# Holding back loads by TensorE progress, and moving transposes to the DMA queues, in a linear-attention and SwiGLU kernel

## The chip, the cores and the metric

One core of one Trainium2 chip runs the whole program. The metric is device microseconds of one execution. The kernel before takes 787.03 us (median of 3 runs, 786.19 to 787.52). Different chips of the same kind gave the same kernel 788.6 to 790.0 us, so every experiment is compared with runs of the kernel before made on the same chip beside it.

## The reference, cut to what matters

```python
xn = layernorm(x)                      # x: 2048 x 1024
# A: linear attention, 32 heads of 32
q, k, v = split(xn @ wqkv)
pq, pk = phi(q), phi(k)                # phi(t) = t + 1 or exp(t), + 1e-6
kv, z = pk^T v, sum(pk)
s = ((pq kv) / (pq z)) @ wo
# B: SwiGLU, 1024 -> 3584 -> 1024
g = silu((silu(xn @ w_gate) * (xn @ w_up)) @ w_down)
return x + s * g
```

The tolerance is not an issue here.

## The kernel before

TensorE computes the large products by a seven-product scheme on 2x2 blocks, so VectorE (DVE) has to form sums of weight blocks ("combinations") before the products, and DVE and ScalarE (ACT) have to empty PSUM, the memory that takes TensorE's products, between them. All instructions are first recorded as operations with their regions. A planner then simulates the five engines and a DMA model and writes each engine's instruction stream in the simulated order. That order is fixed: each engine executes its own stream in order, so an instruction that waits holds everything behind it on that engine. The queue on SyncE (SP), which issues all DMAs, is such a stream too.

The parts that the change touches, with cuts marked:

```python
# Planner: deadline of each op, and the DMA model of the simulation
for o in reversed(ops):
    d = o.pecum if o.eng == "pe" else o.pecum + 30.0     # pecum: TensorE work recorded before it
    for s in o.succs:
        extra = (2.5 + o.nbytes / 250e3) if o.sem is not None else o.busy + o.lat
        d = min(d, s.dl - extra)
    o.dl = d - o.urgent
...
    b = max(s + 0.7, dma_free)
    dma_free = b + o.nbytes / 300e3
    o.done = dma_free + 1.4

# stage 1: each of 16 x tiles (128 x 1024) is normalised, then transposed by TensorE
def t_tile(i):
    ...
    pe_tr([s.r, ident_r], [bank_r[MISC]], trs)           # 8 transposes of 128x128
    act([bank_r[MISC]], [xt_r(i)], dst, pb[:, :, :], ACT.Identity)

# last stage, 8 sets: g*s is 128 columns x 512 tokens, transposed before it is added to x
def turn():
    pe_tr([g.r, ident_r], [bank_r[MISC]], ...)           # 4 transposes of 128x128
    tt([bank_r[MISC], q.r], [q.r], xv[...], pb, xv[...], ALU.add)
    ...                                                  # store when both halves are there
defer(2, turn)

# after the second gate/up pair: 1/denominator is stored to r_scratch, read back
# broadcast in rows of 256 elements, and multiplied into all 16 tiles of phi(q) at once
if (k, n) == ("g", 1):
    recip(p)
    normalise(p)
```

Of the kernel before, what the change touches and what calls it, by code (L numbers as in the profile page):

```python
# [8 lines left out]
ACT = mybir.ActivationFunctionType  # L9
# [4 lines left out]
KB = 1024  # L14
# [15 lines left out]
class Plan:  # L30
# [3 lines left out]
    ENGS = ("pe", "act", "dve", "pool", "sp")  # L34
    LAT = {"pe": 0.22, "act": 0.2, "dve": 0.2, "pool": 0.2}

    def __init__(self, window):
        self.ops = []
        self.lastw = {}
        self.readers = {}  # L40
        self.pecum = 0.0
        self.window = window

    def op(self, eng, reads, writes, fn, busy, sem=None, nbytes=0, urgent=0.0, cow=None):

        o = Op()
        o.eng, o.fn, o.busy, o.sem, o.nbytes, o.urgent = eng, fn, busy, sem, nbytes, urgent
        o.lat = 0.0 if sem is not None else self.LAT[eng]
        o.idx = len(self.ops)
        preds = set()  # L50
        for r in reads:
            for k in r.keys:
                preds.update(self.lastw.get(k, ()))
        if cow is not None:
            preds.update(cow.preds)
        for r in writes:
            for k in r.keys:
                if cow is None:
                    preds.update(self.lastw.get(k, ()))
                    preds.update(self.readers.get(k, ()))  # L60
        for r in reads:
            for k in r.keys:
                self.readers.setdefault(k, []).append(o)
        for r in writes:
            for k in r.keys:
                if cow is None:
                    self.lastw[k] = [o]
                    self.readers[k] = []
                else:
                    self.lastw[k].append(o)  # L70
        o.preds = preds
        o.succs = []
        for p in preds:
            p.succs.append(o)
        o.pecum = self.pecum
        if eng == "pe":
            self.pecum += busy
        self.ops.append(o)
        return o

    def schedule(self):
        ops = self.ops
        for o in reversed(ops):
            d = o.pecum if o.eng == "pe" else o.pecum + 30.0
            for s in o.succs:
                extra = (2.5 + o.nbytes / 250e3) if o.sem is not None else o.busy + o.lat
                d = min(d, s.dl - extra)
            o.dl = d - o.urgent
        for o in ops:
            o.npred = len(o.preds)  # L90
            o.ready = 0.0
# [10 lines left out]
        while len(order) < total:  # L102
# [26 lines left out]
            o.start = s  # L129
            if o.sem is not None:  # L130
                free[e] = s + 0.08
                b = max(s + 0.7, dma_free)
                dma_free = b + o.nbytes / 300e3
                o.done = dma_free + 1.4
            else:
                free[e] = s + o.busy
                o.done = s + o.busy + o.lat
# [65 lines left out]
    return last  # L203


def build_kernel(nc, A_x, A_wqkv, A_wo, B_w_gate, B_w_up, B_w_down, out, WINDOW=6, NWARM=14):
    S, D, FF = 2048, 1024, 3584
    NT, KT, NG, NPAIR = 16, 8, 8, 14
    EPS_LN, EPS_PHI = 1e-5, 1e-6
# [9 lines left out]
    with ExitStack() as es:  # L219
# [42 lines left out]
        m_scr = nc.dram_tensor("m_scratch", [D, D], FP16)  # L262
        m_v = m_scr.rearrange("(g p) c -> p g c", p=128)
        q_scr = nc.dram_tensor("q_scratch", [2, 2, 2, 128, 4 * 512], FP16)
        r_scr = nc.dram_tensor("r_scratch", [2, 4, 32, 256], BF16)

        ps = [es.enter_context(nc.psum_tensor("ps%d" % b, [128, 512], F32)) for b in range(8)]
        bank_r = [named("bank", b) for b in range(8)]
# [17 lines left out]
                semn[name] = sem("d_" + name)  # L286
            return semn[name]

        PL = Plan(WINDOW)
        MM = 0.2137  # L290

        def mm_cost(mms):
# [21 lines left out]
        def tt(reads, writes, o, a, b, op, fast=False):  # L314
            return dve(reads, writes, lambda h: h.tensor_tensor(o, a, b, op), nel(o), 1.92 if fast else 0.96)  # L315

        def dma(reads, writes, o, i, s, nbytes, cow=None):
            return PL.op("sp", reads, writes, lambda h: h.dma_start(o, i), 0.08, sem=s, nbytes=nbytes, cow=cow)  # L318

        class Ring:  # L320
            def __init__(self, arena, off, size, n):
# [59 lines left out]
        rr_ring = Ring(TM, 18 * KB, 2 * KB, 3)  # L381
        fin_ring = Ring(TM, 10 * KB, 1 * KB, 8)
        xo_ring = Ring(TM, 18 * KB, 2 * KB, 3)
        x_ring = Ring(W, 32 * KB, 2 * KB, 4)
        xn_ring = Ring(W, 40 * KB, 2 * KB, 2)
        pk_ring = Ring(W, 44 * KB, 2 * KB, 2)
# [44 lines left out]
        def x_load(i):  # L431
            s = x_ring.take()
            xslot[i] = s
            dma([], [s.r], s.ap(), xf[i * 128:(i + 1) * 128, :], dsem("x%d" % s.k), 256 * KB)

        def wkv_load(c):
            dma([], [wkv_r[c]], wkv[c], wqkv_v[:, :, 1024 + c * 512:1024 + (c + 1) * 512], dsem("wkv%d" % c), 1024 * KB)
# [28 lines left out]
        def t_tile(i):  # L466
            s = xnslot[i]
            xa = s.ap(FP16)
            ar, j, m = xt_dest(i)
            pb = ps[MISC][:, :].bitcast(FP16).rearrange("p (k t) -> p k t", t=128)  # L470
            trs = [(pb[:, kt, :], xa[:, kt * 128:(kt + 1) * 128], ident[:, :]) for kt in range(KT)]
            pe_tr([s.r, ident_r], [bank_r[MISC]], trs)
            dst = ar.at(j * 8 * KB, 8 * KB, FP16).rearrange("p (k t) -> p k t", t=512)[:, :, m * 128:(m + 1) * 128]
            act([bank_r[MISC]], [xt_r(i)], dst, pb[:, :, :], ACT.Identity)
# [287 lines left out]
        def recip(p):  # L762

            flush()
            db = den[p][0]
            e = rr_ring.take()
            ea, ra, rb = e.ap(F32, 0, KB), e.ap(F32, KB, KB), e.ap(BF16, 0, KB // 2)
            er, rr = e.sub(0, KB).r, e.sub(KB, KB).r
            dve([bank_r[db]], [er], lambda h: h.tensor_scalar(ea, ps[db][:, 0:256], 16.0, EPS_PHI, ALU.mult, ALU.add), 256)
            rearm(db)  # L770
            for q in range(4):
                dve([er], [e.sub(KB + q * 256, 256).r], lambda h, q=q: h.reciprocal(
                    ra[:, q * 64:q * 64 + 64], ea[:, q * 64:q * 64 + 64]), 400)
            act([rr], [er], rb, ra, ACT.Identity, "sb")
            dma([er], [named("rscr", p)], r_scr[p].rearrange("q h t -> (q h) t"), rb, dsem("rs"), 64 * KB)

        RB0 = 68 * KB

        def normalise(p):

            for j in range(2):
                rb = H.at(RB0 + j * 8 * KB, 8 * KB).rearrange("p (g q t) -> p g q t", g=NG, q=2)
                rbr = H.reg(RB0 + j * 8 * KB, 8 * KB)
                first = None
                for hl in range(4):
                    rows = r_scr[p, 2 * j:2 * j + 2, :, :].rearrange("q (g h) t -> h g q t", h=4)[hl]
                    for q in range(2):
                        o0 = dma([named("rscr", p)], [rbr], rb[32 * hl:32 * hl + 32, :, q, :],
                                 rows[:, q, :].partition_broadcast(32), dsem("rr%d_%d_%d" % (j, hl, q)), 128 * KB, first)
                        first = first or o0  # L790
                for g in range(NG):
                    src, sr = pq_tile(g, j)
                    dst = src.bitcast(FP16)
                    o = RB0 + j * 8 * KB + g * KB
                    zr, zrr = H.at(o, KB), H.reg(o, KB)
                    act([z_r, zrr], [zrr], zr, zr, ACT.Identity, "sb", scale=zc[:, g:g + 1])
                    tt([sr, zrr], [sr], dst, src, zr, ALU.mult, True)
            for j in range(2):
                for k in range(2):
                    o = PQ0 + (2 * k + j) * 4 * KB  # L800
                    dma([H.reg(o, 4 * KB)], [named("q", p, k, j)], q_scr[p, k, j], H.at(o, 4 * KB, FP16),
                        dsem("pq%d%d" % (k, j)), 512 * KB)


        HB = 6 * KB
# [11 lines left out]
        def gu_load(n):  # L817
            return wload([wg_v[:, :, n * 256:(n + 1) * 256], wu_v[:, :, n * 256:(n + 1) * 256]])

        def gu_pair(p, n, stat):  # L820
            sgs = {}

            def ev_g(i, j, ap, r, bank):
# [4 lines left out]
            def ev_u(i, j, ap, r, bank):  # L828
                s = sgs[i, j]
                o, orr = hb(n, "R%d%d" % (i, j))  # L830
                tt([r, s.r], [orr], o, ap, s.ap(FP16), ALU.mult)
            run_pair(xset(stat, 0, XV[p], ev_g, d_ring), xset(stat, 1, XV[p], ev_u, d_ring))
            if n % 2 == 1:
                v = {nm: hb2(n - 1, nm) for nm in HOF}
                tt([v["R11"][1], v["R01"][1]], [v["T3"][1]], v["T3"][0], v["R11"][0], v["R01"][0], ALU.subtract, True)
# [67 lines left out]
        def d_set(p, c, Sx, mstat, first):  # L903
            gv, sv, xo = {}, {}, {}

            def fin(i, j):
# [11 lines left out]
                q, seen = xo[j]  # L918
                xv = q.ap().rearrange("p (m n) -> p m n", n=256)

                def turn():
                    half = tcnt[0] % 2
                    tcnt[0] += 1
                    pb = ps[MISC][:, half * 256:half * 256 + 256].bitcast(FP16).rearrange("p (m n) -> p m n", n=128)
                    pe_tr([g.r, ident_r], [bank_r[MISC]], [(pb[:, m, :], g.ap(FP16)[:, m * 128:(m + 1) * 128], ident[:, :])
                                                           for m in range(4)])
                    tt([bank_r[MISC], q.r], [q.r], xv[:, :, i * 128:i * 128 + 128], pb[:, :, :],
                       xv[:, :, i * 128:i * 128 + 128], ALU.add)
                    seen.append(i)
                    if len(seen) == 2:  # L930
                        dma([q.r], [], of[row:row + 512, c * 256:(c + 1) * 256].rearrange(
                            "(m p) n -> p m n", p=128), xv, dsem("oo%d" % q.k), 256 * KB)
                defer(2, turn)

            def keep(store, func):
                def f(i, j, ap, r, bank):
# [59 lines left out]
        for p in range(2):  # L996
            for k, n in order:
# [1 line left out]
                if k == "q":  # L999
                    q_pair(p, n, st, ((1, kv_done), (9, kvt)) if (p, n) == (0, 0) else ())  # L1000
                else:
                    gu_pair(p, n, st)
                pump(2)
                if p == 0 and n < 2 and k == "g":
                    for _ in range(8):
# [1 line left out]
                            m_build(*mb.popleft())  # L1007
                if (k, n) == ("g", 1):
                    recip(p)
                    normalise(p)  # L1010
            pq_load(p)
            for c in range(4):
                Sx = wd_load(c)
# [76 lines left out]
```

## Time and profile before

| | before |
|---|---|
| time, median of 3 | 787.03 us |
| span of the profiled run | 787.9 us |
| TensorE busy | 763.0 us, 97% |
| matmuls and transposes on TensorE | 3818 |
| granted TensorE clock, mean | 0.999 |

From the page of the kernel before: busy time by engine, then busy tenths in 40 slices of the span (one digit per 19.7 us), then the chain of work that ended last.

```profile
PE 763.0 (97%) x3818; PEld 347.7 (44%) x3818; DVE 513.2 (65%) x945; ACT 305.0 (39%) x507; POOL 11.5 (1%) x33
PE   8999999999999999999999999999999999999997
DVE  5587432768597766886365676788776768557353
DMA  9921000232883233370633623279423242251510
PE 81%; DMA 10%; ACT 4%; DVE 3%; SPq 2%; issue 1%; ACTq 0%
```

TensorE is the limit. Busy time alone can't say how much is left to win, because matmuls overlap in their records: each 128x512 matmul is shown as 379 ns, though the next starts 216 ns later. So I priced TensorE by start-to-start distances in the records: 216 ns for a matmul of 512 columns, 56 ns for a 128x128 transpose, 59 ns for 129 columns, 219 ns for two 32-row denominator matmuls side by side. The sum is **P = 752.3 us**. The span is then 1.4 us before the first matmul, P, the **gaps G = 30.8 us** (first matmul to last, less P), and 3.4 us after the last.

From the waits of the kernel before (engine, line, what was waited for: us in total, times, longest):

```profile
DVE W L315 <- DMA W<-in_B_w_down_dram: 34.3, 8, 7.7
DVE W L315 <- DMA W<-in_B_w_up_dram: 25.0, 8, 4.8
PE ps L195 <- DVE ps L315: 5.5, 6, 1.4
PE ps L195 <- ACT ps L308: 4.1, 3, 1.5
```

DVE stands 59 us behind weight loads. That is harmless as long as nothing behind it in the stream is wanted. From the timeline (start us, duration us, and in brackets the idle time before and what ended it), one place where something was:

```profile
672.63 5.13 PE L195 MATMUL ps<-H,W 128*128 128x512 f16 x23
677.19 1.28 DVE L315 TENSOR_TENSOR W<-W 128x896 f16<-128x896 bf16 x2 [3.63 <-DMA W<-in_B_w_down_dram]
678.39 0.69 DVE L315 TENSOR_TENSOR ps<-ps,TM 128x512 f32<-128x512 f32 x1
679.14 1.69 PE L195 MATMUL ps<-H,W 128*128 128x512 f16 x7 [1.38 <-DVE ps L315]
```

DVE waited 3.63 us for a load of w_down to form a combination that was wanted only later; the PSUM addition behind it in the stream came late, and TensorE stood 1.38 us for that addition.

Two more places. Near 40 us TensorE waits for a transpose of an x tile that was loaded late, because weight loads filled the queues (DMA share 0.98 and 0.93): the load of x tile 4 was issued at 29.2 us and landed at 36.5 us. And the normalisation: DVE and ACT work through 16 tiles in a lump near 213 to 228 us and again near 530 us. First a line of the timeline, then rows of the windows view (stretch, its length, busy us and count of each engine, granted clock, DMA share, GB/s):

```profile
41.33 0.62 PE L202 MATMUL ps<-ident,W 128*128 128x128 f16 x8 [1.32 <-DVE veps L449]
```

```profile
0.00:20.00 20.00, 16.58 (x83) 7.45 (x84) 11.14 (x26) 6.85 (x9) 4.39 (x20) 1.00 0.98 310
20.00:40.00 20.00, 20.00 (x117) 9.96 (x114) 10.61 (x24) 7.57 (x13) 0.91 (x2) 1.00 0.93 268
...
195.00:250.00 55.00, 51.84 (x242) 22.83 (x241) 42.60 (x77) 31.55 (x58) 0.00 (x0) 1.00 0.67 179
```

### The profile page before, as it was taken

The numbers are of one execution on the slowest core, as the hardware profiler recorded it, in microseconds if no ns is written. First come the engines' busy times: TensorE is split into PE (matmuls) and PEld (weight loads), VectorE is DVE, ScalarE is ACT, GpSimd is POOL, SyncE is SP. The second block draws the span as 40 slices with busy tenths as digits, with TensorE's granted clock in tenths as the row PEclk, the third lists the DMA queues.
The fourth block names the chain that finished last, engine by engine and source line by source line (L and its number), as shares of the span: only waits on it lengthen the run. The fifth ranks groups of instructions, "written<-read, shape, count | busy, mean of one in ns | idle before, by whom it ended". The sixth has DMA issues, their size and how long they took to land.

```text
span 787.9 us, 9684 instructions
## 1 busy us (share of the span) xinstructions
PE 763.0 (97%) x3818; PEld 347.7 (44%) x3818; DVE 513.2 (65%) x945; ACT 305.0 (39%) x507; POOL 11.5 (1%) x33
## 2 busy tenths in 40 slices
PE   8999999999999999999999999999999999999997
PEld 3445555444434444444444444344444444444443
DVE  5587432768597766886365676788776768557353
ACT  3344443555573334322222245547333332232131
POOL 2020000000000000000000000000000000000000
PEclk9999999999999999999999999999999999999999
DMA  9921000232883233370633623279423242251510
GB/s 310 277 67 41 1 1 1 81 107 63 190 246 106 73 89 106 94 222 9 197 92 82 183 71 96 66 156 296 143 63 106 76 126 62 59 171 50 154 41 27
DMA packets 142893, 86.74 MB, mean 110 GB/s; under 512 B 3328, under 2 KB 138752, under 8 KB 142848
## 3 DMA queue, kind: packets, MB, share of 16 engines
q1 hardware_dynamic: 142848, 86.13, 38.8%
q8 instruction: 30, 0.49, 0.3%
q14 instruction: 15, 0.12, 0.1%
HBM read 75.50 MB, written 10.62 MB: 109 GB/s over the span
## 4 chain that ended last, share of the span: by engine, by line
PE 81%; DMA 10%; ACT 4%; DVE 3%; SPq 2%; issue 1%; ACTq 0%
PE ps L195 79%; DMA W<-m_scratch 4%; ACT H L308 2%; PE ps L202 2%; SPq L318 2%; DMA H<-in_A_wqkv_dram 1%; DMA W<-in_B_w_down_dram 1%; DMA H<-r_scratch 1%; DVE W L315 1%; DMA W<-in_B_w_up_dram 1%; ACT TM L308 1%; DVE ps L315 1%; DMA m_scratch<-H 0%; DVE TM L315 0%; ACT ps L308 0%
## 5 line engine op out<-in xcount | busy, mean ns | idle before, releaser
L195 PE MATMUL ps<-X,W 128*128 128x512 f16 x1504 | 346.7, 379 | 7.7 <-DVE TM L315 2.8
L308 ACT ACTIVATE TM<-ps 128x512 f32<-128x512 f32 (+2 forms) x300 | 177.0, 596 | 302.6 <-PE ps L195 302.2
L195 PEld LDWEIGHTS ps<-X,W 128*128 128x128 f16 (+1 forms) x1504 | 143.4, 98 | 184.5 <-DVE ps L315 5.7
L315 DVE TENSOR_TENSOR W<-W 128x1024 f16<-128x1024 bf16 (+3 forms) x224 | 137.3, 629 | 73.2 <-DMA W<-in_B_w_down_dram 34.3
L195 PE MATMUL ps<-H,W 128*128 128x512 f16 x672 | 153.3, 379 | 4.2 <-DVE ps L315 4.0
L195 PE MATMUL ps<-P,W 128*128 128x512 f16 x512 | 122.9, 379 | 1.5 <-ACT ps L308 1.5
L195 PEld LDWEIGHTS ps<-H,W 128*128 128x128 f16 (+1 forms) x672 | 64.7, 98 | 82.2 <-DVE ps L315 7.1
L315 DVE TENSOR_TENSOR ps<-ps,TM 128x512 f32<-128x512 f32 x80 | 55.6, 695 | 69.5 <-PE ps L195 69.5
L315 DVE TENSOR_TENSOR TM<-ps,TM 128x512 f32<-128x512 f32 (+1 forms) x112 | 68.2, 610 | 36.5 <-PE ps L195 27.0
L308 ACT ACTIVATE ps<-ps 128x512 f32<-128x512 f32 x80 | 47.0, 587 | 101.2 <-PE ps L195 101.0
L195 PEld LDWEIGHTS ps<-P,W 128*128 128x128 f16 (+1 forms) x512 | 49.2, 98 | 60.8 <-ACT ps L308 2.0
L315 DVE TENSOR_TENSOR H<-ps,TM 128x512 f16<-128x512 f32 x84 | 57.4, 685 | 4.7 <-PE ps L195 3.3
L195 PE MATMUL ps<-H,X 128*128 128x512 bf16 x256 | 57.3, 379 | 2.6 <-ACT X L308 1.8
L195 PE MATMUL ps<-H,P 128*128 128x512 bf16 x256 | 56.6, 379 | 0.0
L308 ACT ACTIVATE TM<-TM 128x512 f16<-128x512 f32 (+1 forms) x54 | 33.5, 620 | 56.6 <-DVE TM L315 56.4
L315 DVE TENSOR_TENSOR H<-H 128x1024 f16<-128x1024 f16 (+1 forms) x74 | 41.6, 571 | 12.2 <-ACT H L308 11.2
L494 DVE TENSOR_SCALAR TM<-TM 128x512 f16<-128x512 f16 x64 | 17.9, 290 | 41.6 <-ACT TM L308 41.1
L195 PEld LDWEIGHTS ps<-H,X 128*128 128x128 f16 x256 | 24.4, 98 | 31.0 <-ACT X L308 2.1
L195 PEld LDWEIGHTS ps<-H,P 128*128 128x128 f16 x256 | 24.7, 98 | 28.3
L315 DVE TENSOR_TENSOR W<-H 128x1024 f16<-128x1024 f16 x38 | 25.4, 685 | 0.5
L308 ACT ACTIVATE H<-H,zc 128x512 bf16<-128x512 bf16 x32 | 20.8, 716 | 5.0 <-DMA H<-r_scratch 5.0
L495 DVE SCALAR_TENSOR_TENSOR W<-ps,TM 128x512 bf16<-128x512 f32 x32 | 22.0, 688 | 0.8
(60 smaller groups left out, 307.9 us busy)
## 6 DMA issues: line engine op xcount, KB each, us to landing
W<-in_B_w_gate_dram SPq DMA_DIRECT2D x28, 512.0 KB, 3.9
W<-in_B_w_up_dram SPq DMA_DIRECT2D x28, 512.0 KB, 5.2
W<-in_B_w_down_dram SPq DMA_DIRECT2D x16, 896.0 KB, 7.1
W<-in_A_x_dram SPq DMA_DIRECT2D x16, 256.0 KB, 4.1
H<-in_A_wqkv_dram SPq DMA_DIRECT2D x4, 1024.0 KB, 8.8
W<-in_A_wqkv_dram SPq DMA_DIRECT2D x8, 512.0 KB, 7.5
TM<-in_A_x_dram SPq DMA_DIRECT2D x16, 256.0 KB, 4.2
H<-r_scratch SPq DMA_DIRECT2D x32, 128.0 KB, 4.2
```

The costliest lines, as they stand in the source:

```text
L195: last = h.matmul(o, l, r, start=st, stop=sp, skip_group_check=True)
L202: last = h.transpose(o, i, ident)
L308: return PL.op("act", reads, writes, lambda h: h.activation(o, i, func, **kw), nel(o) / 1200.0 + (0.055 if src == "ps" else 0.095))
L315: return dve(reads, writes, lambda h: h.tensor_tensor(o, a, b, op), nel(o), 1.92 if fast else 0.96)
L318: return PL.op("sp", reads, writes, lambda h: h.dma_start(o, i), 0.08, sem=s, nbytes=nbytes, cow=cow)
L494: dve([e.r], [b.r], lambda h: h.tensor_scalar(ba, ea, 1.0, EPS_PHI, ALU.min, ALU.add), 512, 2.6)
L495: dve([src_r, b.r], [out_r], lambda h: h.scalar_tensor_tensor(out_ap, src, 0.0, ba, ALU.max, ALU.add), 512)
```

## The change

The intent: take TensorE off work that the DMA queues can do, and let loads be issued by TensorE's progress instead of as early as a buffer allows. It has five parts.

```diff
 # 1. planner model: a DMA is assumed slower
-                extra = (2.5 + o.nbytes / 250e3) if o.sem is not None else ...
+                extra = (4.0 + o.nbytes / 200e3) if o.sem is not None else ...
-                b = max(s + 0.7, dma_free)
-                dma_free = b + o.nbytes / 300e3
-                o.done = dma_free + 1.4
+                b = max(s + 1.0, dma_free)
+                dma_free = b + o.nbytes / 230e3
+                o.done = dma_free + 1.8
 # 2. holding back: a DMA waits for the TensorE op that lies LEAD = 12 us before its deadline
+        for o in ops:
+            if o.sem is not None and o.succs:
+                k = bisect_right(cum, o.dl - self.lead) - 1
+                if k >= 0 and pes[k] not in o.preds:
+                    o.preds.add(pes[k])
 #    and x loads get a deadline 10 us earlier
-            dma([], [s.r], s.ap(), xf[...], dsem(...), 256 * KB)
+            dma([], [s.r], s.ap(), xf[...], dsem(...), 256 * KB).urgent = 10.0
 # 3. x tiles 4 to 15: DMA transpose
+            if i >= 4:
+                PL.op("sp", [s.r], [xt_r(i)], lambda h: h.dma_start_transpose(dst, xa), ...)
+                return
 # 4. output products of all sets but the last: DMA transpose, then an add from SBUF
+                    PL.op("sp", [g.r], [o.r], lambda h: h.dma_start_transpose(oa, g.ap(FP16)), ...)
+                    tt([o.r, q.r], [q.r], xv[...], oa, xv[...], ALU.add, True)
...
+                if (p, c) == (1, 3):
+                    defer(2, turn)
+                else:
+                    turn_dma()
 # 5. normalisation: four parts over gate/up pairs 2 and 3, rows of 512 elements;
#    the loads of its rows wait for the TensorE op recorded just before them
-                    normalise(p)
+                    if 2 <= n <= 3:
+                        at = tuple((4 + 6 * h, partial(normalise_part, p, n - 2, h)) for h in range(2))
```

More of the change, by code (lines that the diff above doesn't have):

```diff
@@ L1 @@
+from bisect import bisect_right
 from collections import deque
@@ L35, with __init__ @@
     LAT = {"pe": 0.22, "act": 0.2, "dve": 0.2, "pool": 0.2}
-    def __init__(self, window):
+    def __init__(self, window, lead):
         self.ops = []
@@ L42, in __init__, with op @@
         self.window = window
-    def op(self, eng, reads, writes, fn, busy, sem=None, nbytes=0, urgent=0.0, cow=None):
+        self.lead = lead
+    def op(self, eng, reads, writes, fn, busy, sem=None, nbytes=0, urgent=0.0, cow=None, after=None):
         o = Op()
@@ L55, in op @@
             preds.update(cow.preds)
+        if after is not None:
+            preds.add(after)
         for r in writes:
@@ L77, in op @@
             self.pecum += busy
+            self.lastpe = o
         self.ops.append(o)
@@ L85, in schedule @@
             for s in o.succs:
-                extra = (2.5 + o.nbytes / 250e3) if o.sem is not None else o.busy + o.lat
+                extra = (4.0 + o.nbytes / 200e3) if o.sem is not None else o.busy + o.lat
                 d = min(d, s.dl - extra)
             o.dl = d - o.urgent
+        pes = [o for o in ops if o.eng == "pe"]
+        cum = [o.pecum + o.busy for o in pes]
+        for o in ops:
[3 more added lines that the diff above has]
+                    o.preds.add(pes[k])
+                    pes[k].succs.append(o)
         for o in ops:
@@ L203, in _tr_group, with build_kernel @@
     return last
-def build_kernel(nc, A_x, A_wqkv, A_wo, B_w_gate, B_w_up, B_w_down, out, WINDOW=6, NWARM=14):
+def build_kernel(nc, A_x, A_wqkv, A_wo, B_w_gate, B_w_up, B_w_down, out, WINDOW=6, NWARM=14, LEAD=12.0):
     S, D, FF = 2048, 1024, 3584
@@ L264, in build_kernel @@
         q_scr = nc.dram_tensor("q_scratch", [2, 2, 2, 128, 4 * 512], FP16)
-        r_scr = nc.dram_tensor("r_scratch", [2, 4, 32, 256], BF16)
+        r_scr = nc.dram_tensor("r_scratch", [2, 2, 32, 512], BF16)
         ps = [es.enter_context(nc.psum_tensor("ps%d" % b, [128, 512], F32)) for b in range(8)]
@@ L287, in dsem @@
             return semn[name]
-        PL = Plan(WINDOW)
+        PL = Plan(WINDOW, LEAD)
         MM = 0.2137
@@ L315, in tt, with dma @@
             return dve(reads, writes, lambda h: h.tensor_tensor(o, a, b, op), nel(o), 1.92 if fast else 0.96)
-        def dma(reads, writes, o, i, s, nbytes, cow=None):
-            return PL.op("sp", reads, writes, lambda h: h.dma_start(o, i), 0.08, sem=s, nbytes=nbytes, cow=cow)
+        def dma(reads, writes, o, i, s, nbytes, cow=None, after=None):
+            return PL.op("sp", reads, writes, lambda h: h.dma_start(o, i), 0.08, sem=s, nbytes=nbytes, cow=cow,
+                         after=after)
         class Ring:
@@ L383, in build_kernel @@
         xo_ring = Ring(TM, 18 * KB, 2 * KB, 3)
+        pt_ring = Ring(TM, 24 * KB, 1 * KB, 2)
         x_ring = Ring(W, 32 * KB, 2 * KB, 4)
@@ L433, in x_load @@
             xslot[i] = s
-            dma([], [s.r], s.ap(), xf[i * 128:(i + 1) * 128, :], dsem("x%d" % s.k), 256 * KB)
+            dma([], [s.r], s.ap(), xf[i * 128:(i + 1) * 128, :], dsem("x%d" % s.k), 256 * KB).urgent = 10.0
         def wkv_load(c):
@@ L469, in t_tile @@
             ar, j, m = xt_dest(i)
+            if i >= 4:
+                dst = ar.at(j * 8 * KB, 8 * KB, FP16).rearrange("p (k t) -> p k t", t=512)[:, :, m * 128:(m + 1) * 128]
+                PL.op("sp", [s.r], [xt_r(i)], lambda h: h.dma_start_transpose(dst, xa), 0.08, sem=dsem("tx%d" % (i % 2)),
+                      nbytes=400 * KB)
+                return
             pb = ps[MISC][:, :].bitcast(FP16).rearrange("p (k t) -> p k t", t=128)
@@ L774, in recip @@
             act([rr], [er], rb, ra, ACT.Identity, "sb")
-            dma([er], [named("rscr", p)], r_scr[p].rearrange("q h t -> (q h) t"), rb, dsem("rs"), 64 * KB)
-        RB0 = 68 * KB
-        def normalise(p):
-            for j in range(2):
-                rb = H.at(RB0 + j * 8 * KB, 8 * KB).rearrange("p (g q t) -> p g q t", g=NG, q=2)
-                rbr = H.reg(RB0 + j * 8 * KB, 8 * KB)
-                first = None
-                for hl in range(4):
-                    rows = r_scr[p, 2 * j:2 * j + 2, :, :].rearrange("q (g h) t -> h g q t", h=4)[hl]
-                    for q in range(2):
-                        o0 = dma([named("rscr", p)], [rbr], rb[32 * hl:32 * hl + 32, :, q, :],
-                                 rows[:, q, :].partition_broadcast(32), dsem("rr%d_%d_%d" % (j, hl, q)), 128 * KB, first)
-                        first = first or o0
-                for g in range(NG):
-                    src, sr = pq_tile(g, j)
-                    dst = src.bitcast(FP16)
-                    o = RB0 + j * 8 * KB + g * KB
-                    zr, zrr = H.at(o, KB), H.reg(o, KB)
-                    act([z_r, zrr], [zrr], zr, zr, ACT.Identity, "sb", scale=zc[:, g:g + 1])
-                    tt([sr, zrr], [sr], dst, src, zr, ALU.mult, True)
-            for j in range(2):
-                for k in range(2):
-                    o = PQ0 + (2 * k + j) * 4 * KB
-                    dma([H.reg(o, 4 * KB)], [named("q", p, k, j)], q_scr[p, k, j], H.at(o, 4 * KB, FP16),
-                        dsem("pq%d%d" % (k, j)), 512 * KB)
@@ new lines, in recip, with normalise_part @@
+            o0 = None
+            for q in range(4):
+                t0 = (q % 2) * 256
+                o1 = dma([er], [named("rscr", p)], r_scr[p, q // 2, :, t0:t0 + 256], rb[32 * q:32 * q + 32, :],
+                         dsem("rs%d" % q), 16 * KB, o0)
+                o0 = o0 or o1
+        RB0 = 68 * KB
+        def normalise_part(p, j, half):
+            o = RB0 + (2 * j + half) * 4 * KB
+            rb, rbr = H.at(o, 4 * KB).rearrange("p (g t) -> p g t", t=512), H.reg(o, 4 * KB)
+            first = None
+            for hl in range(4):
+                rows = r_scr[p, j].rearrange("(g h) t -> h g t", h=4)[hl, 4 * half:4 * half + 4]
+                o0 = dma([named("rscr", p)], [rbr], rb[32 * hl:32 * hl + 32, :, :], rows.partition_broadcast(32),
+                         dsem("rr%d_%d_%d" % (j, half, hl)), 128 * KB, first, PL.lastpe)
+                first = first or o0
+            for gl in range(4):
+                g = 4 * half + gl
+                src, sr = pq_tile(g, j)
+                dst = src.bitcast(FP16)
+                zr, zrr = H.at(o + gl * KB, KB), H.reg(o + gl * KB, KB)
+                act([z_r, zrr], [zrr], zr, zr, ACT.Identity, "sb", scale=zc[:, g:g + 1])
+                tt([sr, zrr], [sr], dst, src, zr, ALU.mult, True)
+            o = PQ0 + (2 * half + j) * 4 * KB
+            dma([H.reg(o, 4 * KB)], [named("q", p, half, j)], q_scr[p, half, j], H.at(o, 4 * KB, FP16),
+                dsem("pq%d%d" % (half, j)), 512 * KB)
@@ L818, in gu_load, with gu_pair @@
             return wload([wg_v[:, :, n * 256:(n + 1) * 256], wu_v[:, :, n * 256:(n + 1) * 256]])
-        def gu_pair(p, n, stat):
+        def gu_pair(p, n, stat, at=()):
             sgs = {}
@@ L831, in ev_u @@
                 tt([r, s.r], [orr], o, ap, s.ap(FP16), ALU.mult)
-            run_pair(xset(stat, 0, XV[p], ev_g, d_ring), xset(stat, 1, XV[p], ev_u, d_ring))
+            run_pair(xset(stat, 0, XV[p], ev_g, d_ring), xset(stat, 1, XV[p], ev_u, d_ring), at)
             if n % 2 == 1:
@@ L919, in fin, with done, turn_dma @@
                 xv = q.ap().rearrange("p (m n) -> p m n", n=256)
+                def done():
+                    seen.append(i)
+                    if len(seen) == 2:
+                        dma([q.r], [], of[row:row + 512, c * 256:(c + 1) * 256].rearrange(
+                            "(m p) n -> p m n", p=128), xv, dsem("oo%d" % q.k), 256 * KB)
+                def turn_dma():
+                    o = pt_ring.take()
+                    oa = o.ap(FP16).rearrange("p (m n) -> p m n", n=128)
+                    PL.op("sp", [g.r], [o.r], lambda h: h.dma_start_transpose(oa, g.ap(FP16)), 0.08,
+                          sem=dsem("tp%d" % o.k), nbytes=200 * KB)
+                    tt([o.r, q.r], [q.r], xv[:, :, i * 128:i * 128 + 128], oa, xv[:, :, i * 128:i * 128 + 128], ALU.add,
+                       True)
+                    done()
                 def turn():
@@ L928, in turn @@
                        xv[:, :, i * 128:i * 128 + 128], ALU.add)
-                    seen.append(i)
-                    if len(seen) == 2:
-                        dma([q.r], [], of[row:row + 512, c * 256:(c + 1) * 256].rearrange(
-                            "(m p) n -> p m n", p=128), xv, dsem("oo%d" % q.k), 256 * KB)
-                defer(2, turn)
+                    done()
+                if (p, c) == (1, 3):
+                    defer(2, turn)
+                else:
+                    turn_dma()
             def keep(store, func):
@@ L1001, in build_kernel @@
                 else:
-                    gu_pair(p, n, st)
+                    at = ()
+                    if 2 <= n <= 3:
+                        at = tuple((4 + 6 * h, partial(normalise_part, p, n - 2, h)) for h in range(2))
+                    gu_pair(p, n, st, at)
                 pump(2)
```

## The prediction

> **What bounds it now.** TensorE: the page shows it 97% busy over a 787.9 us span, granted clock 0.999; the chain of waits is 81% TensorE. In the instruction records successive 128x512 matmuls start 216 ns apart, 128x128 transposes 56 ns. Pricing every matmul so gives about 752 us. The rest: 1.4 us before the first matmul, 3.4 us after the last, about 31 us of gaps. Of the gaps 4.6 us fall in the first 25 us; 2.3 us around 40 us (a transpose waits for a late x tile; DMA share 0.95 up to there); about 5 us at 213-228 and 530 us (normalisation: DVE and ACT work through r_scratch products while PSUM evictions wait); about 6 us around the small denominator matmuls; 4.4 us at transposes of output products; most of the remainder where in-order DVE stood behind a weight load (it waited 34 us for w_down, 25 us for w_up) and evicted late.
>
> **What the change does.**
> 1. 12 of 16 x tiles lose 8 TensorE transposes each, 28 of 32 output products 4 each: 208 x 56 ns = 11.7 us, all on the critical path. Sure gain.
> 2. The turn gaps outside the last set go: 2.5 us.
> 3. Weight loads held back free the DMA queues for x in the first 40 us: the 2.3 us gap goes. The start itself stays.
> 4. Normalisation is cut into four parts over two weight pairs, with 1024-byte rows in place of 512: 3 of its 5 us.
> 5. The planner's slower DMA model places DVE's weight combinations later in its order: perhaps 2 us.
>
> **What it adds.** 12 DMA transposes of 256 KB and 28 of 128 KB, 6.7 MB beside 86 MB. The Trainium skill ("Advanced Engine Details and Errata", X-Bar Transpose) expects 350-400 GB/s of them; no run here shows one yet. Estimate from the trace: packets up to 512 bytes take 27 ns; 64 packets of 256 bytes on each of 16 engines is 1.7 us for an x tile, plus about 2.5 us that small transfers show from issue to landing: 4 us, and 3.5 us for a product. An x tile has over 7 us of matmuls ahead of it, so its latency is hidden. The products' adds sit in DVE's in-order stream: where a transpose lands later than planned, DVE blocks and evictions slip; loads behind a transpose in the in-order queue wait for its product. I charge 3 us for this and for held-back loads that come late.
>
> **Sum.** 787 - 11.7 - 2.5 - 2.3 - 3 - 2 + 3, about 768.5 us; range 759 to 780. Faster by over 2% (below 771.3): 0.62; within 2%: 0.35; slower: 0.03.
>
> **What would show the steps right.** TensorE instructions fall by 208, clock unchanged; the gaps' sum falls from 31 to roughly 24 us; DVE waits on w_down and w_up fall from 59 us together to under 40; DMA share before 40 us falls; the gap near 40 us is gone; TensorE waits under 1 us for DMA-transposed x; transposes land in 3 to 5 us.
>
> **What would make it wrong.** DMA transposes that land in 8 us or more, or slow other transfers beside them: DVE waits for them appear in the output stages (about 330-420 and 660-790 us) with new TensorE gaps, and the gain shrinks to 5 us or none. Loads held back too far: waits on weights grow in the gate/up stages. Gaps that merely move: only the 11.7 us arrive, 775 us. If the gaps fall by more than 15 us, the time is below 760.

## More of the kernel before

G counts waits and matmuls that run at a lower clock. The document uses P and G for each kernel; they are worked out, not printed by any view.

## The result, and the profile after

The changed kernel takes **763.32 us** (median of 3 runs, 763.12 to 765.06), against 787.03. The ratio is 0.9707, 95% interval 0.9681 to 0.9732. A ratio is the mean time of one kernel's fast runs over that of the other's in the same rounds, so not quite the ratio of the medians. A second measurement on another chip gave 762.40 us and 0.9664 (0.9639 to 0.9688): two measurements of the same pair can differ by 0.4%, and I read nothing smaller out of comparisons between chips. All outputs are right.

| | before | after |
|---|---|---|
| span of the profile | 787.9 | 763.1 (second profile 760.4) |
| TensorE weight loads recorded (one for each matmul) | 3818 | 3610 |
| P, priced TensorE work | 752.3 | 740.6 |
| G, gaps from first to last matmul | 30.8 | 17.6 (second profile 14.9) |
| DVE waits for w_down and w_up | 59.3 | 0.5 |

So of 24.8 us of span, 11.7 us are work that TensorE no longer does and 13.2 us are gaps. (15 matmul records are missing from this trace, so P of after is P of before less 208 x 56 ns.)

From the page of the kernel after, the lines that answer to those above:

```profile
PE 748.0 (98%) x3595; PEld 338.8 (44%) x3610; DVE 517.6 (68%) x945; ACT 296.9 (39%) x497; POOL 11.9 (2%) x33
PE   6999999999999999999999999999999999999997
DVE  4665623868798677785574868788877778565463
DMA  9333314525385332543547554246732336337740
PE 95%; ACT 2%; DVE 1%; DMA 1%; issue 0%; SPq 0%
```

DMA fell from 10% to 1% of the chain that ended last. Waits of the kernel after:

```profile
DVE TM L329 <- DMA TM<-TM: 18.2, 10, 6.3
DVE W L329 <- DMA W<-in_B_w_up_dram: 0.5, 1, 0.5
PE ps L209 <- DMA H<-in_A_wqkv_dram: 2.2, 1, 2.2
PE ps L209 <- DVE ps L329: 1.1, 2, 0.6
```

The DVE waits for weights are gone; new ones stand for transposed products (TM<-TM), up to 6.3 us, and yet TensorE waited only 1.1 us for DVE's additions. Windows of the kernel after, for comparison with the rows above:

```profile
0.00:20.00 20.00, 13.64 (x65) 6.30 (x67) 8.38 (x20) 6.04 (x7) 4.49 (x20) 0.91 0.88 287
20.00:40.00 20.00, 19.89 (x110) 9.81 (x110) 14.06 (x35) 7.10 (x12) 2.99 (x5) 1.00 0.29 68
...
195.00:250.00 55.00, 55.00 (x257) 24.95 (x255) 45.10 (x78) 31.41 (x55) 0.00 (x0) 1.00 0.64 187
```

The DMA share between 20 and 40 us fell from 0.93 to 0.29, x tile 4 landed at 21.1 us instead of 36.5, the gap near 40 us is gone, and from 195 to 250 us TensorE has no gap. But the first 20 us got worse. Timeline of TensorE after:

```profile
7.62 0.62 PE L216 MATMUL ps<-ident,W 128*128 128x128 f16 x8 [1.62 <-DVE W L470]
10.40 2.92 PE L209 MATMUL ps<-H,X 128*128 128x512 bf16 x8 [2.15 <-DMA H<-in_A_wqkv_dram]
```

The first projection matmul waited 2.15 us for its weight and ran at half clock (8 matmuls in 2.92 us where they took 1.90 us before). Two things delayed that weight: the urgency puts the second x tile ahead of it (0.7 us), and in this profile one of the 16 DMA engines landed its share 3.5 us after the first engine. In the second profile that spread was 1.6 us, in the kernel before 0.5 us.

From the list of DMA issues after (last number: median us from issue to landing), the transposes:

```profile
TM<-TM SPq DMA_TRANSPOSE x28, 2.9
P<-W SPq DMA_TRANSPOSE x8, 3.1
X<-W SPq DMA_TRANSPOSE x4, 3.1
```

### The profile page after: what moved, and what is told of

Its sections match the earlier page's. It is cut to its first block, busy times and chain, and to the rows that moved or that the text cites. A ratio compares the mean times of both kernels' runs of the same rounds, so it can differ in the third digit from the quotient of the medians.

```text
span 763.1 us, 9351 instructions
## 1 busy us (share of the span) xinstructions
PE 748.0 (98%) x3595; PEld 338.8 (44%) x3610; DVE 517.6 (68%) x945; ACT 296.9 (39%) x497; POOL 11.9 (2%) x33
## 4 chain that ended last, share of the span: by engine, by line
PE 95%; ACT 2%; DVE 1%; DMA 1%; issue 0%; SPq 0%
PE ps L209 95%; DMA H<-in_A_wqkv_dram 1%; ACT H L322 0%; PE ps L216 0%; ACT TM L322 0%; DVE TM L329 0%; ACT L322 0%; DVE W L329 0%; DVE ps L329 0%; ACT ps L322 0%; ACT X L322 0%; SPq L332 0%; DVE H L606 0%; DVE H L516 0%; DVE zc L601 0%
## 5 line engine op out<-in xcount | busy, mean ns | idle before, releaser
L209 PE MATMUL ps<-H,W 128*128 128x512 f16 x672 | 150.6, 379 | 1.4 <-ACT TM L322 1.4
L329 DVE TENSOR_TENSOR W<-W 128x1024 f16<-128x1024 bf16 (+3 forms) x224 | 133.9, 628 | 4.7 <-PE ps L209 2.3
L329 DVE TENSOR_TENSOR TM<-ps,TM 128x512 f32<-128x512 f32 (+1 forms) x84 | 56.7, 675 | 55.4 <-PE ps L209 52.6
L329 DVE TENSOR_TENSOR TM<-TM 128x512 f16<-128x512 f16 (+1 forms) x60 | 25.1, 420 | 29.5 <-DMA TM<-TM 18.2
```

Of the source, the lines that this page charges most:

```text
L209: last = h.matmul(o, l, r, start=st, stop=sp, skip_group_check=True)
L329: return dve(reads, writes, lambda h: h.tensor_tensor(o, a, b, op), nel(o), 1.92 if fast else 0.96)
```

## The experiments

**Theory A.** Half of the gain is TensorE work that the transposes save, 11.7 us, with or without the rest; the other half is gaps that close because the new planning stops DVE and the SP queue from standing behind loads. **Rival B.** The transposes carry nearly all of the gain. **Rival C.** The new planning carries it and the transposes alone cost as much as they save.

### Each part alone, and all but the transposes

b_tr adds parts 3 and 4 to the kernel before:

```diff
 # kernel before
+            if i >= 4:   (DMA transpose of x, as in the change)
+                    turn_dma()   (DMA transpose of products, as in the change)
```

> The kernel before plus the DMA transposes alone (12 x tiles, 28 output products); no holding back, old planner model, old normalisation. Theory A (half of the gain is TensorE issue, half is gaps closed by the new planning): 208 x 56 ns = 11.7 us go, and some 2.5 us of turn waits, so about 773 us. Rival B (the transposes carry nearly all of it): about 765 us. Rival C (without the new planning the transposes cost as much as they save): 780 us or more.

a_pe_tr puts every transpose of the kernel after back on TensorE:

```diff
 # kernel after
-            if i >= 4:
+            if i >= NT:
-                if (p, c) == (1, 3):
+                if p >= 0:
```

> The kernel after with every transpose back on TensorE; holding back, new planner model and new normalisation kept. Theory A: 763.3 + 11.7 + about 2 us of turn waits, so about 777 us. Rival B: about 787 us, nothing left of the gain. Rival C: about 777 us too; it differs from A in the run before.

b_hold_model adds parts 1 and 2 to the kernel before, without the urgency:

```diff
 # kernel before
+  the slower DMA model (part 1); +  o.preds.add(pes[k]) with LEAD = 12.0 (part 2)
```

> The kernel before plus the holding back of loads and the slower planner model, nothing else. Theory A: DVE waits for w_down and w_up fall from 59 us to under 15 us and 5 to 8 us of TensorE gaps go, so 779 to 782 us. Rival B: 786 to 788 us, the waits of DVE were off the critical path.

b_norm adds part 5 to the kernel before:

```diff
 # kernel before
-                    normalise(p)
+                    normalise_part(p, n - 2, h) at two points of pairs 2 and 3; r_scratch rows of 512
```

> The kernel before plus the new normalisation alone (four parts, 1024-byte rows). Theory A: the gaps of about 5 us at 213-228 us and 530 us go, so 782 to 784 us. Rival B: 786 to 788 us; other gaps take their place because DVE still stands behind loads.

Measured on one chip, kernel before at 788.67 us:

| run | time | ratio (95%) | P | G |
|---|---|---|---|---|
| b_tr | 784.84 | 0.9948 (0.9923 to 0.9974) | 740.6 | 37.8 |
| a_pe_tr | 775.51 | 0.9837 (0.9808 to 0.9865) | 752.3 | 16.2 |
| b_hold_model | 785.10 | 0.9960 (0.9935 to 0.9985) | 752.3 | 26.0 |
| b_norm | 788.68 | 1.0000 (0.9970 to 1.0029) | 752.3 | 29.0 |

The transposes alone won only 4 us. They saved their 11.7 us of TensorE work, and 7 us came back as gaps. The largest is at x tile 4. (The next, near 710 us, is of the kind seen in the kernel before: DVE waits 5.64 us for a load of W from m_scratch, TensorE 2.30 us behind it, and the clock is halved for 3.4 us.) Timeline of b_tr, and two windows:

```profile
41.36 1.32 SPq L473 DMA_TRANSPOSE X<-W  x1
44.58 4.02 PE L195 MATMUL ps<-H,X 128*128 128x512 bf16 x9 [3.58 <-DMA X<-W]
```

```profile
40.00:45.00 5.00, 1.12 (x12) 0.62 (x11) 4.47 (x14) 0.23 (x1) 1.86 (x4) 0.76 0.47 93
45.00:50.00 5.00, 5.00 (x15) 1.85 (x14) 2.45 (x7) 0.60 (x1) 0.00 (x0) 0.56 1.21 193
```

The x tile is as late as before, since weight loads are still issued ahead of it; now 3 us of transpose latency come on top, TensorE waits 3.58 us, and then the granted clock is halved (0.76 and 0.56 in the two windows; the profile's list of clock changes gives 6.8 us at half speed, from 42.6 to 49.4 us). The Trainium skill says this in "TensorE: Matmul & The Clock Gate", section "Why this matters for your kernels": no idle gaps above about 3 us, or the clock falls back to half. This stall agrees; shorter ones brought the clock down too, as the 2.30 us above, so the 3 us are no safe bound here (see the last section). Matmuls ran at half clock from 44.6 to 49.4 us, which lost about 2.4 us more (half of 4.8), so the stall of 3.58 us cost about 6 us in this execution. The drop is not the same in each: the mean clock of b_tr's four runs was 0.993, 0.994, 0.997 and 0.998.

The planning without the transposes won 13 us, nearly all of it gaps (30.8 to 16.2). That is against rival B, and b_tr is against theory A's 773 us: it lies in rival C's range (780 us or more), though its gain of 4 us is clear of noise. Yet from a_pe_tr to the kernel after (ratios 0.9837 against 0.9664 and 0.9707) it is another 10 to 14 us, the full price of the transposes. So the transposes are worth 4 us with the old planning and about 12 with the new. The parts need each other: b_tr, b_hold_model and b_norm together lower the median by 7.4 us (3.8 + 3.6 + 0.0), all parts at once by 23.7; only the urgency of the x loads is in none of the three. So theory A had the two halves right and was wrong that they are independent.

b_norm shows no gain in time: DVE still stood 57 us behind w_down and w_up. So rival B (786 to 788 us) came nearest for b_norm. In b_hold_model those waits fell to 2.5 us, as expected, but two stalls of the normalisation grew, to 2.34 us near 231 us and 2.62 us near 548 us, and each was followed by 3.4 us at half clock. The first:

```profile
231.00 5.31 PE L205 MATMUL ps<-X,W 128*128 128x512 f16 x16 [2.34 <-DVE ps L325]
```

The 16 matmuls took 5.31 us where 16 at full clock take about 3.6. Theory A was some 3 to 5 us too hopeful in both runs. My reading is that each run removes one of two stalls that take turns; that the two together, in a_pe_tr, leave no gap over 0.7 us between 200 and 350 us fits it, but no run shows the turn-taking itself.

### The kernel after, less one part

```diff
 # a_nohold
-LEAD=12.0
+LEAD=1e9
 # a_oldmodel: part 1 undone, part 2 kept
-extra = (4.0 + o.nbytes / 200e3);  b = max(s + 1.0, ...);  o.nbytes / 230e3;  dma_free + 1.8
+extra = (2.5 + o.nbytes / 250e3);  b = max(s + 0.7, ...);  o.nbytes / 300e3;  dma_free + 1.4
 # a_oldnorm: part 5 undone
 # a_nourg: the urgency of the x loads undone
-... 256 * KB).urgent = 10.0
+... 256 * KB)
```

> The kernel after without the holding back (every load may issue as soon as its buffer is free); planner model, normalisation and DMA transposes kept. Theory A2 (the transposes pay only where the loads are held back, because a transpose and its source queue behind early weight loads): x tile 4 is late again near 40 us, TensorE stands for over 3 us there and the granted clock halves for some us; 770 to 776 us. Rival B2 (the slower planner model alone places DVE's work well): 763 to 766 us.

> The kernel after with the old, faster planner model of a DMA; loads still held back. Theory A2: loads are held back from deadlines that are now some 2 us too late and DVE's order expects them early, so DVE waits for loads and transposes come back (over 30 us together against 18 us for the transposes now) and the time is 766 to 770 us. Rival B2 (the model is the main thing): 772 us or more. Rival C2 (12 us of lead cover it): 762 to 765 us.

> The kernel after with the old normalisation in one lump and 512-byte rows. Theory A2 (cutting it is worth nothing beside other stalls, as the run with it alone showed, but is the last stall of the gate and up stages once loads are held back, as the lumps of 2.5 and 2.8 us with holding back alone showed): gaps of 2 to 4 us near 225 us and 530 us, 768 to 772 us. Rival B2 (worth nothing anywhere): 763 to 765 us.

> The kernel after without the 10 us of urgency of the x loads, so that the first projection weight goes out before the second x tile. Theory A2: the first matmul of the projection waits 0.7 us or more less and the clock stays up in the first 20 us; 1 to 3 us faster than the kernel after on the same chip, 760.5 to 762.5 us. Rival B2 (later x tiles come late and their transposes with them): 765 us or more.

Measured on one chip, kernel before at 790.02 us. P is 740.6 in all; the kernel after has ratios 0.9664 and 0.9707 and G of 14.9 and 17.6, so each loss of G in this section is counted from 17.6 and from 14.9.

| run | time | ratio (95%) | G |
|---|---|---|---|
| a_nohold | 772.47 | 0.9791 (0.9754 to 0.9827) | 25.2 |
| a_oldmodel | 779.19 | 0.9876 (0.9837 to 0.9915) | 31.9 |
| a_oldnorm | 771.18 | 0.9762 (0.9734 to 0.9790) | 22.6 |
| a_nourg | 765.73 | 0.9684 (0.9656 to 0.9712) | 18.5 |

Without the holding back, x tile 4 is late again, though the urgency was kept (it landed at 37.1 us); without the urgency, in a_nourg, nothing stalls near 40 us. So it is the holding back that closes this gap. The timeline of a_nohold has the stall of b_tr in the same place:

```profile
46.32 4.02 PE L209 MATMUL ps<-H,X 128*128 128x512 bf16 x9 [4.38 <-DMA X<-W]
```

Nine matmuls in 4.02 us: half clock again. This one place, with about 2.7 us lost to the clock, explains 7 of the 8 to 10 us of G; the DVE waits for w_down stayed at 4.7 us, so the slower model, not the holding back, is what removes them. That splits the two halves of the planning: the holding back is worth its time at the start, the model in the later stages.

Undoing the model was the largest loss of the four, 14 to 17 us of G, and above what theory A2 expected (766 to 770 us): rival B2, that the model is the main thing (772 us or more), was right here. Waits of a_oldmodel:

```profile
DVE TM L329 <- DMA TM<-TM: 32.4, 17, 3.6
DVE W L329 <- DMA W<-in_B_w_down_dram: 17.3, 10, 4.4
DVE W L329 <- DMA W<-m_scratch: 11.3, 5, 3.6
DVE W L329 <- DMA W<-in_B_w_up_dram: 11.2, 6, 3.6
PE ps L209 <- DVE ps L329: 8.1, 8, 2.9
```

And one place in its timeline, where DVE stands behind a load and TensorE behind DVE:

```profile
219.79 1.90 DVE L329 TENSOR_TENSOR W<-W 128x1024 f16<-128x1024 bf16 x3 [3.09 <-DMA W<-in_B_w_up_dram]
...
223.75 0.69 DVE L329 TENSOR_TENSOR ps<-ps,TM 128x512 f32<-128x512 f32 x1
...
224.50 3.84 PE L209 MATMUL ps<-X,W 128*128 128x512 f16 x17 [2.94 <-DVE ps L329]
```

The old normalisation, which was worth nothing when changed alone, costs 5 to 8 us of G here, as theory A2 expected: stalls of 2.35 us near 222 us and 2.62 us near 536 us, the second followed by 3.4 us at half clock. The first took no clock with it, though it was of the same length as the first one in b_hold_model above.

a_nourg can't be told from the kernel after by its time. Its start is different, not better: with two weights ahead of the second x tile, TensorE waits 2.9 us for that tile's transposes, and the clock halves for 3.4 us where theory A2 had it stay up. Theory A2 was wrong about it.

### Why the model matters, the exceptions, and a better version

```diff
 # a_oldmodel_lead20: a_oldmodel with
-LEAD=12.0
+LEAD=20.0
 # a_all_tr: every transpose on DMA
-            if i >= 4:
+            if i >= 0:
-                if (p, c) == (1, 3):
+                if p < 0:
 # a_best: the start order of the kernel before, and one denominator group for each query pair
-... 256 * KB).urgent = 10.0
+... 256 * KB).urgent = 1.0
+                    pend.append((g, j, o, orr))
+                    if len(pend) < 8:
+                        return
                     def den_mm():      # now the 16 matmuls of all 8 tiles in pend, in one op
                         ...
                     defer(7, den_mm)
 # after_again: the kernel after, unchanged
```

> The kernel after as it is, as the yardstick for the next run on the same chip: ratio to the kernel before 0.969 to 0.973. If the late DMA engine at the start of its first profile (3.5 us between the first and the last engine of a projection weight) was chance, the start of this profile shows under 1 us there.

> The kernel after with the old planner model of a DMA, but a lead of 20 us in place of 12. It asks why the old model cost so much with the loads held back. Theory A3 (loads came late for their deadlines): the 8 us of extra lead cure it, 764 to 768 us, and DVE waits for weights all but vanish. Rival B3 (the order of DVE's instructions is planned for transfers that land too early, the lead does not matter): 774 us or more, and DVE waits for transposes stay near 32 us.

> The kernel after with every transpose on DMA, the first four x tiles and the last set too. Theory A3 (a DMA transpose pays only where its latency of some 3 us is covered, and it stands in the queue behind loads issued before it): TensorE issue falls by another 48 x 56 ns = 2.7 us, but the first projection matmul starts 5 us or more later, with the clock halved, and the end grows by 1 to 2 us; 767 to 776 us. Rival B3 (the exceptions were needless): 760 to 762 us.

> The kernel after with the x loads' urgency at 1 us (which gives the start order of the kernel before: x, weight, x, weight, weight, x) and with the denominator matmuls gathered into one group for each pair of query weights. Theory A3: about 1 us at the start, and of the 6.2 us of gaps around the 32 small groups most of the part before each group, 3 to 5 us together; 757 to 761 us where the kernel after takes 763 to 765. Rival B3: the gap stays with each pair of small matmuls even in a group, so only the start is won: 762 to 764 us.

Measured on one chip, kernel before at 788.57 us:

| run | time | ratio (95%) | P | G | after the last matmul |
|---|---|---|---|---|---|
| after_again | 762.40 | 0.9664 (0.9639 to 0.9688) | 740.6 | 14.9 | 3.4 |
| a_oldmodel_lead20 | 775.05 | 0.9819 (0.9792 to 0.9845) | 740.6 | 27.9 | 3.4 |
| a_all_tr | 779.27 | 0.9872 (0.9841 to 0.9902) | 737.9 | 26.3 | 12.0 |
| a_best | 754.88 | 0.9566 (0.9542 to 0.9591) | 740.6 | 7.8 | 3.4 |

after_again missed both of its expectations narrowly: the ratio lies below 0.969, and the landings of the first projection weight spread over 1.6 us where under 1 us was expected. (No one engine is far behind the others there, so the late engine of the first profile was not seen again; why the spread stays wider than before is open.)

**The model.** Eight more microseconds of lead take back 4 us of G and leave 13 us more than the kernel after has. So loads that come late for their deadlines are not the main cause. What remains is the order: with the old model the planner believes that transfers land sooner than they do and places DVE's combinations where it believes them ready; DVE then stands. The traces bear this out. In DVE's stream, counted in instructions, 176 of the 224 combinations of weight blocks stand earlier in a_oldmodel_lead20 than in the kernel after, and 10 later. Measured by the count of matmuls that TensorE has reached (one as 0.205 us), loads of w_down go out about 4 us sooner than in the kernel after, and DVE forms its combinations about 5 us sooner (medians): the longer lead brought the wish forward with the load. With the lead of 12 us both causes are at work: 83 combinations stand earlier (7 later), and loads of w_down go out about 3 us later than in the kernel after, as the old deadlines have it. The waits for transposes did not stay near 32 us as rival B3 said. The time (775.05 us) is in rival B3's range, but these waits fell to 8.3 us, and those for w_down rose from 17.3 to 36.7 us:

```profile
DVE W L329 <- DMA W<-in_B_w_down_dram: 36.7, 8, 8.9
PE ps L209 <- DVE ps L329: 9.2, 9, 2.9
```

The waits move between transfers, the loss stays. I did not separate the three constants of the model, nor the deadline's constant from the simulation's; that is open.

**The exceptions.** With all transposes on DMA the time is 779.27 us, worse than I expected of it. At the start, the first x transpose is queued behind three weight loads of 1 MB and lands 10 us after its issue; TensorE waits 13.6 us, and the clock is at half for 17 us. At the end nothing covers the latency: 12.0 us pass after the last matmul, with the last products still to be transposed, against 3.4. Waits and end of the timeline of a_all_tr:

```profile
PE ps L209 <- DMA X<-W: 13.6, 1, 13.6
```

```profile
764.81 1.21 PE L209 MATMUL ps<-W 128*128 128x512 f16 x4
...
768.35 4.86 SPq L952 DMA_TRANSPOSE TM<-TM  x3
...
774.51 0.42 DVE L329 TENSOR_TENSOR TM<-TM 128x512 bf16<-128x512 f16 x1 [1.79 <-DMA TM<-TM]
```

The last 48 transposes would save 2.7 us of TensorE work and cost some 20 us of exposed latency. The exceptions in the change are needed.

**The better version.** a_best beats both kernels: 754.88 us, 1.0% below the kernel after on the same chip. Its start was not better (gaps of 6.1 us in the first 25 us against 6.0), so that half of theory A3 failed: now TensorE waits 1.5 us for the second x tile, whose normalisation stands in DVE's stream behind an operation that waits 2.0 us for ACT. All of the gain came from gathering the denominator matmuls, and it is more than I expected. TensorE's timeline in after_again, then in a_best:

```profile
145.46 0.28 PE L209 MATMUL ps<-H,Zh 128*32 128x256 bf16 x2
145.68 1.04 PE L209 MATMUL ps<-X,W 128*128 128x512 f16 x4
146.65 0.29 PE L209 MATMUL ps<-H,Zh 128*32 128x256 bf16 x2
```

```profile
142.81 6.85 PE L209 MATMUL ps<-X,W 128*128 128x512 f16 x31
149.59 0.63 PE L209 MATMUL ps<-H,Zh 128*32 128x256 bf16 x16
150.15 2.12 PE L209 MATMUL ps<-X,W 128*128 128x512 f16 x9
```

Before, a pair of these matmuls (32 output rows each, side by side in the array) took 0.22 us up to the next matmul, and some 0.09 us more were lost ahead of it. In the group, 8 pairs take 0.56 us, 70 ns each. Over 32 pairs that is about 32 x (0.31 - 0.07) = 7.7 us (summed in the traces, 9.98 us before and 2.61 us in the groups), which is the 7.1 us by which G fell, within the accuracy of these numbers. Fewer changes between small and large matmuls are not all of it: in the group the pairs of two token halves run side by side as well, four matmuls starting within 16 ns and the next four some 110 ns later. Two at a time at this spacing, the group would take about 1.0 us (an estimate), so some 1.7 of the 7.4 us come from this, over the four groups.

## Why the prediction was right, point by point

The time lay inside the range (759 to 780), on the side forecast as most likely. The gain was 23.7 us where 18.5 were forecast. The work term was right; the gaps were to fall by 6.8 us net and fell by 13.2 (second profile 15.9), so the range held and the sum did not. The terms were of unequal quality:

1. **TensorE work, 11.7 us.** Confirmed by count: 208 fewer. But "sure gain" was too strong. It is sure as work, not as time: with the old planning only 4 us of it arrived (b_tr).
2. **Turn gaps (TensorE's waits at the transposes of output products), 2.5 us.** Those gaps are gone, but in two sets a wait of 0.85 us stands in their place, so about 1 us of it is real.
3. **The gap near 40 us, 2.3 us.** Gone, and a_nohold shows that the holding back did it, and that it guards more than that: with DMA transposes and without it the stall is 4.4 us and takes the clock with it. "The start itself stays" was wrong: gaps in the first 25 us rose from 4.6 to 6.0 us (8.5 us in the profile with the late DMA engine).
4. **Normalisation, 3 of 5 us.** Under-sized: all 5 us went, and putting the lump back costs 5 to 8 us of G (a_oldnorm).
5. **The planner's DMA model, 2 us.** This is the term that was mis-sized most. Undoing it costs 14 to 17 us of G (a_oldmodel), the largest of all parts. That is what it is worth beside all the others; the losses of single parts overlap, and this one alone is as large as all that the gaps fell by, so no share of the sum can be read from it. DVE waits for weights fell from 59 us to 0.5, where I had put "under 40" as the sign. What failed in my sizing, as I see it: I went by the few TensorE gaps in the trace of before that had a load right ahead of them, and did not see that DMA transposes add transfers that DVE waits for.
6. **Charge of 3 us for late transposes and loads.** DVE does wait for transposed products, 18 us in total, but TensorE shows no gap from it: the charge was not needed with the new planning. With the old planning gaps grew by 7 us (b_tr), about 6 of them at x tile 4, whose latency I had called hidden.

The transposes landed in 2.9 to 3.1 us, as medians (forecast 3 to 5), single ones as late as 7.4 us. The sum of gaps fell from 31 to 17.6 us (forecast 24).

## What to carry to other kernels

Work moved from a full engine to DMA was worth its price here only where the new latency was covered: check the first and the last use, what stands ahead in the queue, and what stands behind the wait in an in-order stream. When a planner fixes the order, its DMA model is part of the performance: one that is too fast placed instructions where their data had not landed, and loads issued sooner did not cure it, because the instructions moved too. Test parts together as well as alone, because a part that is worth nothing alone (the normalisation) can be worth 5 us beside the others.

## What the Trainium skill lacked or had wrong

- "Advanced Engine Details and Errata", X-Bar Transpose, calls DMA transposes as fast as regular DMAs and expects 350-400 GB/s. Here their 256-byte packets took 18 ns on each of 16 engines, worked out 228 GB/s while moving, against 27 ns for 512 bytes, 303 GB/s, for ordinary ones. From issue to landing 128x1024 took 3.1 us, and 128x512 took 2.4 us when nothing stood ahead and up to 7.4 us (8.9 us in the second profile) behind other transfers.
- "VectorE: DVE Perf Modes", The three transpose paths, compares 390 ns (TensorE) with 1309 ns (DMA) for 128x128 and does not say that these are no prices in a stream. In a stream of matmuls TensorE's price was 56 ns a transpose, so the work saved by moving one is about a seventh of what that table suggests.
- No page that I read prices the issue of such a transpose on trn2 in microseconds ("DMA: Bandwidth & Descriptors" has sequencer cycles for the generations before trn3 together): SP was held 1.2 us by most, both for 128x512 and for 128x1024, and up to 4.1 us by one, against about 0.4 us for a plain load that found the queue free.
- "TensorE: Matmul & The Clock Gate" gives about 3 us of idling as what brings the clock down. Here waits of 2.30 us (b_tr) and 2.34 us (b_hold_model) brought it down for 3.4 us, and waits of 2.35 us (a_oldnorm), 2.88 us (b_hold_model) and 2.94 us (a_oldmodel) did not; the kernel after lost it with 2.15 us, 1.62 us of another wait just ahead. Waits of 3.6 and 4.4 us brought it down for 6.8 us.
- The same page gives the gain of packing small matmuls side by side, but not the price of changing between them and full-width ones ("TensorEngine Tiling (Array Packing)" says that a change of mode drains the engine, without a time): a lone pair cost about 0.31 us here, a pair in a group of eight, where four matmuls ran side by side, 0.07 us.
